# Attention before two expert layers: k and f laid out for plain transposes, values two units late

## Chip, core and metric

The kernel runs on one core of one Trainium2 chip. The metric is the device time of one execution in microseconds; for the kernel before it is 927.1 us, the median of three runs (927.02 to 927.17). A TensorE clock of 1.00 in the profile is its 2.4 GHz level, 0.50 its 1.2 GHz level.

## What is computed

Three stages in a row. Only the first is touched, apart from a small piece of work that moves out of the second.

```
f = 1 / (1 + exp(-f_logit))                      # q, k, v, f_logit: 4 batches, 8 heads, 768 steps, 48 wide
for t in range(S):                               # linear attention with a decay per head and row
    state = f[t, :, None] * state + outer(k[t], v[t])
    y[t] = q[t] @ state
logits = x @ w_gate                              # x: 3072 tokens x 384
# routing: all (token, expert) pairs in order of falling logit; a token goes to the
# first expert of its list that has fewer than 384 tokens
out[mask_e] = relu(x[mask_e] @ w1[e]) @ w2[e]    # 8 experts
# then RMS norm and a gated layer: (silu(xn @ w_gate) * (xn @ w_val)) @ w_out
```

## The kernel before

The attention stage takes the first fifth of the time. Its work is cut into 16 units, four per batch; a unit is two heads that share the 128 partitions (head 0 in rows 0 to 47, head 1 in rows 64 to 111). A head's 768 steps are six chunks of 128. The decay is handled by products of f inside a chunk: with P the running product of f and W the factor that belongs to k, the unit needs k scaled by W and q scaled by P, both with the 48 features on the partitions and the steps along the row.

The inputs arrive the other way round: `load` fetches a raw tensor as 96 partitions, each with 8 steps of both heads in contiguous runs of 1536 bytes (`raw_f`, `raw_k`, `raw_q`, three buffers each). `turned` brings them into the needed layout with TensorE: a matmul with the identity for each head and each of the 8 steps, 64 stationary columns (48 and 16 that are not used), 96 moving ones; half of a tensor fills one PSUM bank. Then come, by their names in the code: `decays` (the sigmoid of the turned f, into G and fs), `scans` (VectorE: P and W), `scale` (VectorE: kt and qt out of the turned k and q), `k_back` (five transposes of kt, copied to kn), `inner` (kt times qt for all 12 head chunks, copied to `at` on ScalarE, masked on GpSimd), `sums` (kn times v, copied to ub, state scan on VectorE into st), `values` (state and inner parts multiplied into yp0 and yp1, copied to YT). After four units `logits` and `logits_sum` do the gate. Some of the matmuls use only a part of the array: state products read 48 rows and write 48 columns (48*48 in the profile), inner values 128*48, inner products 48*128, turning 96*64, transposes the whole width.

The order of every engine is the order in which the loop at L509 and below is written out; nothing is reordered. In iteration i it turns q of unit i, runs decays of i + 2, scale and k_back of i, values of i - 1, inner of i, scans of i + 1, sums of i, and at last turns k of unit i + 1. PSUM banks for turned inputs, transposes and inner products come from one pool of five that is used in rotation (`bank()`): a new bank waits until its last reader five allocations ago is done. ScalarE and VectorE work in order, so a copy that waits holds everything behind it. Loads are issued by SyncE, also in order; each waits until its buffer has been read.

Calls in `extra` are put at the head of an iteration: constants for the routing in iteration 2, the preparation of the routing (ranges of the logits so far, two transposes) in iteration 14. In the routing stage that follows, `side` is called in each step; its first call makes more constants on GpSimd (`more_consts`) and then turns one table (`turn_inc`).

Of the kernel before, what the change touches and what calls it, by code (L numbers as in the profile page):

```python
# [63 lines left out]
class Route:  # L64
# [83 lines left out]
    def steps(self, n, rows=None, side=None):  # L148
        nc, NB, E, NA = self.tc.nc, self.NB, self.E, self.NACT
        K, ones = self.K, self.K["ones"]  # L150
        with self.tc.tile_pool(name="r_wk", bufs=2) as wk, self.tc.tile_pool(name="r_ps", bufs=2, space=PSUM) as ps:
            def one(s):
# [48 lines left out]
                if rows and s == 0:  # L201
                    side(-1)
# [103 lines left out]
def attention(tc, q, k, v, f_logit, YT, w_gate, lg, pmin, ident, extra):  # L306
# [18 lines left out]
    NR = dict(f=3, k=3, q=3)  # L325
    RAW = {}
    for nm in "fkq":
        for i in range(NR[nm]):
            t = cst.tile([TP, 2 * R * D + 16], F32, name=f"raw_{nm}{i}")
            nc.gpsimd.memset(t[:, 2 * R * D:], 20.0 if nm == "f" else 0.0)  # L330
            RAW[nm, i] = t
    NV = 4
    V = [cst.tile([128, NC, 2, D], F32, name=f"v{i}") for i in range(NV)]

# [3 lines left out]
    def load(names, i):  # L338
        if not 0 <= i < NU:
            return  # L340
        b, p = units[i]
        for nm in names:
            if nm == "v":
                for h in range(2):
                    nc.sync.dma_start(V[i % NV][:, :, h, :], v[b, 2 * p + h].rearrange("(n p) d -> p n d", p=C))
                continue
            src = dict(f=f_logit, k=k, q=q)[nm]
            nc.sync.dma_start(RAW[nm, i % NR[nm]][:, 0:2 * R * D].rearrange("p (h c) -> p h c", h=2),
                              src[b, 2 * p:2 * p + 2].rearrange("h (p r) d -> p h (r d)", r=R))
# [32 lines left out]

    def turned(nm, i, g):

        t = RAW[nm, i % NR[nm]]
        o = bank()
        for r in range(4):
            for h in range(2):
# [13 lines left out]
    def decays(i):  # L402
        G[i] = wk.tile([128, S + 1], F32, name="G")
        FS[i] = wk.tile([128, NC], F32, name="fs")
        for g in range(2):
            o = turned("f", i, g)
            nc.scalar.activation(tv(G[i][:, :S], g), ov(o), AF.Sigmoid)
            if g == 0:
                nc.scalar.activation(FS[i], o[:, 0:TP:C // R], AF.Sigmoid)
# [17 lines left out]
    def scale(O, X, F, name, i):  # L427
        X[i] = wk.tile([128, S], F32, name=name)
# [12 lines left out]
    def inner(i):  # L441

        AT[i] = wk.tile([128, 2, NC, C], F32, name="at")
# [16 lines left out]
    def sums(i):  # L460
# [6 lines left out]
        ST[i] = wk.tile([128, D, NC], F32, name="st")  # L467
# [41 lines left out]
    for i in range(-2, NU + 1):  # L509
# [12 lines left out]
        if i > -2:  # L522
            load("kq", i + 3)
        if on(i - 1):
            values(i - 1)
# [6 lines left out]
        if on(i - 1) and units[i - 1][1] == NP - 1:  # L532
            for f in (logits, logits_sum):
                for g in range(2):
                    f(units[i - 1][0], g)
        if on(i + 1):
            KO[i + 1] = [turned("k", i + 1, g) for g in range(2)]
        if i == NU - 2:
# [153 lines left out]
def tile_kernel(ctx, tc, q, k, v, f_logit, w_gate, w1, w2, w2_gate, w2_val, w2_out, rms_g, out):  # L692
# [39 lines left out]
    def prepare(bank):  # L732
# [8 lines left out]
              {2: lambda bank: K.update(route_consts(tc, rc)), 14: prepare})  # L741
# [58 lines left out]
    with ExitStack() as st:  # L800
        with tc.tile_pool(name="rw", bufs=6) as rw, tc.tile_pool(name="rwp", bufs=4, space=PSUM) as rwp:
# [7 lines left out]
            def side(s):  # L809
                if s < 0:  # L810
                    bank = rwp.tile([128, 4, 2, 64], F32, name="rows").rearrange("p a b c -> p (a b c)")
                    turn_inc(tc, K, bank[:, 0:128], ident)
                    return
                if s == 0:
                    more_consts(tc, rc, K)
# [358 lines left out]
```

## Time and profile before

| | |
|---|---|
| time, median of 3 runs | 927.1 us |
| profiled execution | 926.02 us, span 924.3 us |
| mean granted TensorE clock | 0.968 |
| TensorE busy | 876.3 us (95%) |
| VectorE, ScalarE, GpSimd busy | 502.0, 380.7, 277.3 us |
| attention stage | 0 to about 186 us |
| routing stage, clock at 0.50 | about 192 to 250 us |

The profile is of one execution, 1.1 us shorter than the median run; its span lies 1.7 us under its own time. Rows of the time line give start, length, engine, line, operation, tiles (written <- read), shapes and count, and in brackets the idle time of the engine before the row with what ended it. PE is TensorE's matmuls and PEld its weight loads. An fp32 matmul shows as two records, a transpose as one. Matmul ends are modelled and overlap, so prices are best read from start to start of neighbouring groups.

### The profile page before, as it was taken

The numbers are of one execution on the slowest core, as the hardware profiler recorded it, in microseconds if no ns is written. First come the engines' busy times: TensorE is split into PE (matmuls) and PEld (weight loads), VectorE is DVE, ScalarE is ACT, GpSimd is POOL, SyncE is SP. The second block draws the span as 40 slices with busy tenths as digits, with TensorE's granted clock in tenths as the row PEclk, the third lists the DMA queues.
The fourth block names the chain that finished last, engine by engine and source line by source line (L and its number), as shares of the span: only waits on it lengthen the run. The fifth ranks groups of instructions, "written<-read, shape, count | busy, mean of one in ns | idle before, by whom it ended". The sixth has DMA issues, their size and how long they took to land.

```text
span 924.3 us, 17642 instructions
## 1 busy us (share of the span) xinstructions
PE 876.3 (95%) x7263; PEld 844.5 (91%) x7263; DVE 502.0 (54%) x839; ACT 380.7 (41%) x748; POOL 277.3 (30%) x328
## 2 busy tenths in 40 slices
PE   7999999866699999999999999999999999999997
PEld 7889897755599999999899999999999999999996
DVE  6665666477679888886744333443324333343222
ACT  3444444366245555454752332423324232242221
POOL 3323333154557777773410201102011010100101
PEclk9999999965599999999999999999999999999999
DMA  9556551062567788776320000000000000000000
GB/s 207 122 114 135 110 119 28 1 219 109 190 243 246 248 296 290 266 243 218 104 69 1 26 1 1 27 1 26 1 1 26 1 27 2 1 26 1 26 1 26
DMA packets 70168, 87.73 MB, mean 95 GB/s; under 512 B 29632, under 2 KB 56256, under 8 KB 70080
## 3 DMA queue, kind: packets, MB, share of 16 engines
q1 hardware_dynamic: 61008, 70.00, 26.0%
q0 software_dynamic: 3072, 9.44, 3.1%
q10 hardware_dynamic: 6000, 7.09, 2.2%
q8 instruction: 58, 0.95, 0.4%
q14 instruction: 30, 0.25, 0.1%
HBM read 70.01 MB, written 16.52 MB: 94 GB/s over the span
## 4 chain that ended last, share of the span: by engine, by line
PE 71%; issue 11%; DVE 10%; POOL 3%; DMA 2%; ACT 1%; POOLq 0%; ACTq 0%; SPq 0%; DVEq 0%
PE bank L390 7%; PE yp L484 5%; PE v L574 4%; PE g L573 4%; PE v L573 4%; PE v L572 4%; PE g L574 4%; PE g L572 4%; PE o L573 4%; PE o L572 4%; PE o L574 4%; PE bank L450 3%; PE x L573 2%; PE x L574 2%; PE x L572 2%
## 5 line engine op out<-in xcount | busy, mean ns | idle before, releaser
L1112 DVE TENSOR_TENSOR hf<-sg,v 128x384 f32<-128x384 f32 x96 | 53.1, 553 | 193.8 <-PE v L574 164.6
L900 POOL TENSOR_TENSOR xlo<-xn,xhi 128x384 fp32r<-128x384 f32 x24 | 27.4, 1143 | 302.3 <-ACT xhi L899 302.3
L1115 ACT CAST hh<-hf 128x384 fp32r<-128x384 f32 x96 | 49.3, 513 | 139.0 <-DVE hf L1112 137.3
L573 PE MATMUL o<-w,hh 128*128 128x384 f32 x288 | 97.0, 337 | 0.0
L572 PE MATMUL o<-w,hh 128*128 128x384 f32 x288 | 96.6, 335 | 0.0
L573 PE MATMUL g<-xlo,w 128*128 128x384 f32 x288 | 96.6, 335 | 0.0
L574 PE MATMUL v<-xhi,w 128*128 128x384 f32 x288 | 96.6, 335 | 0.0
L572 PE MATMUL v<-xhi,w 128*128 128x384 f32 x288 | 96.6, 335 | 0.0
L573 PE MATMUL v<-xlo,w 128*128 128x384 f32 x288 | 96.5, 335 | 0.0
L574 PE MATMUL g<-xhi,w 128*128 128x384 f32 x288 | 96.5, 335 | 0.0
L574 PE MATMUL o<-w,hl 128*128 128x384 f32 x288 | 96.3, 334 | 0.0
L572 PE MATMUL g<-xhi,w 128*128 128x384 f32 x288 | 96.2, 334 | 0.0
L1110 ACT ACTIVATE sg<-g 128x384 f32<-128x384 f32 x96 | 47.1, 491 | 118.7 <-PE g L574 118.5
L1116 DVE TENSOR_TENSOR hl<-hf,hh 128x384 fp32r<-128x384 f32 x96 | 53.6, 559 | 55.6 <-ACT hh L1115 55.6
L965 POOL TENSOR_TENSOR nr<-nr,ne 128x384 f32<-128x384 f32 x36 | 62.4, 1734 | 46.5 <-DVE ne L964 17.3
L573 PE MATMUL x<-hl,w 128*128 128x384 f32 x192 | 65.7, 342 | 2.5 <-DVE hl L1037 2.2
L759 DVE TENSOR_TENSOR w<-wraw,w 128x1536 fp32r<-128x1536 f32 x35 | 64.6, 1845 | 5.3 <-ACT w L756 5.2
L572 PE MATMUL h<-xhi,w 128*128 128x384 f32 x192 | 67.1, 349 | 0.3 <-ACT xhi L928 0.3
L573 PE MATMUL h<-xlo,w 128*128 128x384 f32 x192 | 65.7, 342 | 0.0
L574 PE MATMUL h<-xhi,w 128*128 128x384 f32 x192 | 65.5, 341 | 0.0
L572 PE MATMUL x<-hh,w 128*128 128x384 f32 x192 | 65.3, 340 | 0.0
L457 POOL TENSOR_SCALAR_AFFINE_SELECT at<-at 128x384 f32<-128x384 f32 x62 | 31.5, 543 | 111.2 <-ACT at L456 111.1
(231 smaller groups left out, 2034.3 us busy)
## 6 DMA issues: line engine op xcount, KB each, us to landing
wraw<-in_moe_w_dram SPq DMA_DIRECT2D x32, 768.0 KB, 5.9
raw_f<-in_f_logit_dram SPq DMA_DIRECT2D x16, 288.0 KB, 3.4
raw_k<-in_k_dram SPq DMA_DIRECT2D x16, 288.0 KB, 5.0
raw_q<-in_q_dram SPq DMA_DIRECT2D x16, 288.0 KB, 5.0
v<-in_v_dram SPq DMA_DIRECT2D x32, 144.0 KB, 4.6
x_dram<-xrows SPq DMA_DIRECT2D x24, 192.0 KB, 1.9
nraw<-in_moe_w_gate_dram SPq DMA_DIRECT2D x12, 384.0 KB, 5.9
nraw<-in_moe_w_val_dram SPq DMA_DIRECT2D x12, 384.0 KB, 5.2
```

The lines of the kernel that those rows point to most:

```text
L390: nc.tensor.matmul(o[64 * h:64 * h + 64, r * TP:(r + 1) * TP], t[:, c0:c0 + 64], ident[0:TP, 0:TP], start=True, stop=True)
L457: nc.gpsimd.affine_select(out=t, in_=t, pattern=[[0, 3], [1, C]], compare_op=OP.is_ge, fill=0.0, base=0, channel_multiplier=-1)
L484: nc.tensor.matmul(YP[n // 3][d, (n % 3) * C:(n % 3 + 1) * C], ST[i][d, :, n] if state else V[i % NV][:, n, h, :], QT[i][d, c] if state el ...
L572: nc.tensor.matmul(out, lhs[0], rhs[0], start=first, stop=False)
L573: nc.tensor.matmul(out, lhs[0], rhs[1], start=False, stop=False)
L574: nc.tensor.matmul(out, lhs[1], rhs[0], start=False, stop=last)
L759: eng.tensor_tensor(out=lo, in0=raw, in1=hi.bitcast(F32), op=OP.subtract)
L965: nc.gpsimd.tensor_tensor(out=r, in0=r, in1=e2.bitcast(F32), op=OP.mult)
L1110: nc.scalar.activation(sg, pg, AF.Silu)
L1112: nc.vector.tensor_tensor(out=h, in0=sg, in1=pv, op=OP.mult)
L1115: nc.scalar.copy(hh, h)
L1116: nc.vector.tensor_tensor(out=hl, in0=h, in1=hh.bitcast(F32), op=OP.subtract)
```

## The change

f and k get a second layout: 96 partitions with 8 steps, each of 2 heads padded from 48 to 64 elements, so that one step of both heads is 128 columns and one plain transpose turns it. For k the load itself writes that layout (two loads of 192-byte runs, from unit 2 on; units 0 and 1 stay as before). For f the raw load stays, and a new function `relay` on ScalarE copies it through the sigmoid into the padded layout; the copies out of PSUM in `decays` become plain copies. q stays as it was. In the loop, values run for unit i - 2, at the head of the iteration, with all state products first; k and q of unit i + 1 are turned together at its end; decays move behind k_back, loads of k and q are issued one unit earlier, and the loop is one iteration longer. More buffers for qt, at and st go with that. The two small pieces of routing work move from the routing's first step into iterations 4 and 6.

```diff
+    def relay(i):
+        if 0 <= i < NU:
+            nc.scalar.activation(RL["f", i % 2][:, :, :, 0:D].rearrange("p r h d -> p h r d"),
+                                 raw("f", i)[:, 0:2 * R * D].rearrange("p (h r d) -> p h r d", h=2, r=R), AF.Sigmoid)
...
     def turned(nm, i, g):
         o = bank()
         for r in range(4):
+            if padded(nm, i):
+                t = RL[nm, i % (2 if nm == "f" else 3)]
+                nc.tensor.transpose(o[:, r * TP:(r + 1) * TP], t[:, 4 * g + r].rearrange("p h d -> p (h d)"),
+                                    ident[0:TP, 0:TP])
+                continue
...
-            nc.scalar.activation(tv(G[i][:, :S], g), ov(o), AF.Sigmoid)
+            nc.scalar.copy(tv(G[i][:, :S], g), ov(o))
...
-        todo = [(h, n, True) for h, n in ((1, 3), (0, 1), (1, 4), (0, 2), (1, 5))]
+        todo = [(h, n, True) for h, n in ((0, 1), (1, 3), (0, 2), (1, 4), (1, 5), (1, 1), (0, 3), (1, 2), (0, 4), (0, 5))]
         todo += [(h, n, False) for n in range(NC) for h in range(2)]
-        todo += [(h, n, True) for h, n in ((0, 3), (1, 1), (0, 4), (1, 2), (0, 5))]
...
+    relay(0)
+    for i in range(-2, NU + 2):
         if i in extra:
             extra[i](bank()[:, 0:256])
-        if on(i):
-            QO[i] = [turned("q", i, g) for g in range(2)]
-        if on(i + 2):
-            decays(i + 2)
-        load("f", i + 5)
+        if on(i - 2):
+            values(i - 2)
         load("v", i + 2)
         if on(i):
             scale(KO, KT, W, "kt", i)
             scale(QO, QT, P, "qt", i)
             k_back(i)
-        if i > -2:
-            load("kq", i + 3)
-        if on(i - 1):
-            values(i - 1)
+        if on(i + 2):
+            decays(i + 2)
+        load("f", i + 5)
         if on(i):
             inner(i)
         if on(i + 1):
             scans(i + 1)
         if on(i):
             sums(i)
...
         if on(i + 1):
             KO[i + 1] = [turned("k", i + 1, g) for g in range(2)]
+            QO[i + 1] = [turned("q", i + 1, g) for g in range(2)]
+        relay(i + 3)
+        load("kq", i + 4)
...
-              {2: lambda bank: K.update(route_consts(tc, rc)), 14: prepare})
+              {2: lambda bank: K.update(route_consts(tc, rc)), 4: lambda bank: more_consts(tc, rc, K),
+               6: lambda bank: turn_inc(tc, K, bank[:, 0:128], ident), 14: prepare})
```

On TensorE, in the steady part of the loop, before: U is written by sums, kt read by k_back, yp written by values.

```order
L464 MATMUL U<-v_124,kn 48x48 x10
L390 MATMUL bank<-ident,raw_k_110 64x96 x16
L390 MATMUL bank<-ident,raw_q_116 64x96 x16
L390 MATMUL bank<-ident,raw_f_108 64x96 x16
L438 MATMUL bank<-ident,kt 128x128 x5
L484 MATMUL yp_141<-qt,st 48x128
```

And now on TensorE, from the end of values to the next values; rl_f and rl_k are the padded layouts.

```order
L509 MATMUL yp_146<-at,v_127 48x128 x6
L464 MATMUL bank<-ident,kt 128x128 x5
L410 MATMUL bank<-ident,rl_f_107 128x96 x8
L476 MATMUL bank<-qt,kt 128x128 x12
L490 MATMUL U<-v_129,kn 48x48 x10
L410 MATMUL bank<-ident,rl_k_115 128x96 x8
L416 MATMUL bank<-ident,raw_q_121 64x96 x16
L509 MATMUL yp_145<-qt,st 48x128
```

f has moved from ahead of k_back to behind it, values from behind k_back to ahead of it, and k and f are 8 transposes each where they were 16 matmuls.

On ScalarE, one iteration in the steady part, before: G and fs come from decays, kn from k_back, YT from values, at from inner, ub from sums.

```order
L407 ACTIVATE G<-bank 128x96x4
L409 ACTIVATE fs<-bank 128x6
L407 ACTIVATE G<-bank 128x96x4
L439 COPY kn<-bank 128x384
L439 COPY kn<-bank 128x256
L490 COPY YT<-yp_140 112x384
L490 COPY YT<-yp_141 112x384
L456 COPY at<-bank 128x384 x4
L466 COPY ub_153<-U 128x5x48
```

The same on ScalarE now.

```order
L515 COPY YT<-yp_145 112x384
L515 COPY YT<-yp_146 112x384
L465 COPY kn<-bank 128x384
L465 COPY kn<-bank 128x256
L433 COPY G<-bank 128x96x4
L435 COPY fs<-bank 128x6
L433 COPY G<-bank 128x96x4
L482 COPY at<-bank 128x384 x4
L492 COPY ub_159<-U 128x5x48
L401 ACTIVATE rl_f_107<-raw_f_104 96x2x8x48
```

The YT copies stand first instead of behind kn, G and fs come after kn, and the relay is a new last row.

At the end of the loop on TensorE, before: one unit's values stand behind the last sums.

```order
L450 MATMUL bank<-qt,kt 128x128 x12
L464 MATMUL U<-v_125,kn 48x48 x10
L484 MATMUL yp_141<-qt,st 48x128
L484 MATMUL yp_140<-qt,st 48x128
L484 MATMUL yp_141<-qt,st 48x128
```

And now, on TensorE from the last sums to the inner part of the next values.

```order
L476 MATMUL bank<-qt,kt 128x128 x12
L490 MATMUL U<-v_130,kn 48x48 x10
L509 MATMUL yp_145<-qt,st 48x128
L509 MATMUL yp_146<-qt,st 48x128
L509 MATMUL yp_145<-qt,st 48x128
L509 MATMUL yp_146<-qt,st 48x128 x2
L509 MATMUL yp_145<-qt,st 48x128
L509 MATMUL yp_146<-qt,st 48x128
L509 MATMUL yp_145<-qt,st 48x128
L509 MATMUL yp_146<-qt,st 48x128 x2
L509 MATMUL yp_145<-at,v_129 48x128 x6
```

The values behind the last sums are now those of the unit before the last (they read v_129, not v_130), and the last unit's follow them.

## Rows read from the trace of the kernel before

**Rows 1.** Busy time by engine in one stretch: stretch, its length, busy us (instructions).

```profile
60.00:140.00 80.00, 79.85 (x1487) 70.31 (x1482) 51.54 (x74) 37.94 (x96) 26.62 (x48) 1.00 0.52 114
```

**Rows 2.** The chain of waits from 0 to 190 us, its shares by line.

```profile
by line: PE bank L390 31.9%; PE yp L484 26.1%; PE bank L450 12.3%; PE bank L438 5.9%; PE U L464 4.0%; DMA raw_f<-in_f_logit_dram 3.4%; PE bank L496 3.3%; POOL cp L179 1.3%; DVE kt L430 1.3%; PE bank L504 1.2%; ACT lgT L499 1.0%; POOL at L45
```

**Rows 3.** Time line, one unit's weight loads: start us, length us, engine, line.

```profile
118.96 0.53 PEld L438 LDWEIGHTS bank<-ident,kt 128*128 128x128 f32 x5
...
119.66 0.68 PEld L484 LDWEIGHTS yp<-qt,st 48*48 48x48 f32 x10 [0.17 <-issue]
...
120.48 1.26 PEld L484 LDWEIGHTS yp<-at,v 128*48 128x48 f32 x24
...
121.93 0.67 PEld L484 LDWEIGHTS yp<-qt,st 48*48 48x48 f32 x10 [0.18 <-issue]
...
122.75 1.42 PEld L450 LDWEIGHTS bank<-qt,kt 48*128 48x128 f32 x24
...
124.29 0.53 PEld L464 LDWEIGHTS U<-v,kn 128*48 128x48 f32 x20
...
124.73 1.36 PEld L390 LDWEIGHTS bank<-ident,raw_k 96*64 96x64 f32 x32
...
126.03 1.38 PEld L390 LDWEIGHTS bank<-ident,raw_q 96*64 96x64 f32 x32
...
127.35 1.38 PEld L390 LDWEIGHTS bank<-ident,raw_f 96*64 96x64 f32 x32
...
128.85 0.53 PEld L438 LDWEIGHTS bank<-ident,kt 128*128 128x128 f32 x5
```

**Rows 4.** Time line, the routing's first transposes, their weight loads.

```profile
185.90 1.54 PEld L556 LDWEIGHTS rows<-ident,YT 112*128 112x128 f32 x16 [0.59 <-DVE lg L505]
```

**Rows 5.** VectorE from 60 to 140 us: group, count | busy us, mean ns | idle before.

```profile
L417 DVE TENSOR_TENSOR_SCAN P<-G,d 128x768 f32<-128x768 f32 x8 | 14.1, 1758 | 0.3
...
L430 DVE TENSOR_TENSOR kt<-bank,W 128x384 f32<-128x384 f32 x16 | 8.2, 539 | 1.3 <-PE bank L390 1.1
L469 DVE TENSOR_TENSOR_SCAN st<-ub,z 128x288 f32<-128x288 f32 x8 | 7.5, 944 | 26.9 <-ACT ub L466 26.9
```

**Rows 6.** Time line, ScalarE: one G, two kn, two YT copies, one large cast.

```profile
119.08 0.49 ACT L407 ACTIVATE G<-bank 128x384 f32<-128x384 f32 x1
...
119.60 0.75 ACT L439 COPY kn<-bank 128x384 f32<-128x384 f32 x2
...
122.66 0.86 ACT L490 COPY YT<-yp 112x384 f32<-112x384 f32 x2 [2.30 <-PE yp L484]
...
196.79 1.48 ACT L822 CAST w<-wraw 128x1536 fp32r<-128x1536 f32 x1
```

**Rows 7.** DMA issues of the page: count, KB each, median us to landing.

```profile
raw_k<-in_k_dram SPq DMA_DIRECT2D x16, 288.0 KB, 5.0
...
v<-in_v_dram SPq DMA_DIRECT2D x32, 144.0 KB, 4.6
```

**Rows 8.** Time line, TensorE where it waited for VectorE in the attention stage.

```profile
33.63 0.88 PE L390 MATMUL bank<-ident,raw_f 96*64 96x96 f32 x16 [0.63 <-DVE kt L430]
...
171.94 0.74 PE L438 MATMUL bank<-ident,kt 128*128 128x128 f32 x5 [0.59 <-DVE kt L430]
...
179.43 0.89 PE L484 MATMUL yp<-qt,st 48*48 48x128 f32 x10 [1.54 <-DVE st L469]
```

**Rows 9.** The chain of waits, k_back of units 14 and 15: start, us, what.

```profile
151.41 0.70 PE bank L438 x5
...
162.74 0.73 PE bank L438 x5
```

**Rows 10.** Time line, the start on TensorE: f of unit 1, first k_back.

```profile
8.79 2.83 PE L390 MATMUL bank<-ident,raw_f 96*64 96x96 f32 x32 [1.45 <-DMA raw_f<-in_f_logit_dram]
...
16.92 0.77 PE L438 MATMUL bank<-ident,kt 128*128 128x128 f32 x5
```

**Rows 11.** Busy time by engine in the routing stage.

```profile
200.00:210.00 10.00, 5.44 (x68) 4.63 (x68) 7.94 (x29) 7.72 (x21) 5.54 (x6) 0.50 0.65 208
```

More of the change, by code (lines that the diff above doesn't have):

```diff
@@ L323, in attention, with padded, raw @@
     psl = pool("a_psl", 1, space=PSUM)
-    NR = dict(f=3, k=3, q=3)
-    RAW = {}
+    PAD = "k"
+    RAW, RL = {}, {}
     for nm in "fkq":
-        for i in range(NR[nm]):
+        for i in range(2 if nm in PAD else 3):
             t = cst.tile([TP, 2 * R * D + 16], F32, name=f"raw_{nm}{i}")
-            nc.gpsimd.memset(t[:, 2 * R * D:], 20.0 if nm == "f" else 0.0)
+            if nm != "f":
+                nc.gpsimd.memset(t[:, 2 * R * D:], 0.0)
             RAW[nm, i] = t
+        for i in range(3 if nm in PAD else 2 if nm == "f" else 0):
+            t = cst.tile([TP, R, 2, 64], F32, name=f"rl_{nm}{i}")
+            nc.gpsimd.memset(t[:, :, :, D:], 1.0 if nm == "f" else 0.0)
+            RL[nm, i] = t
+    def padded(nm, i):
+        return nm == "f" or nm in PAD and i > 1
     NV = 4
     V = [cst.tile([128, NC, 2, D], F32, name=f"v{i}") for i in range(NV)]
+    def raw(nm, i):
+        return RAW[nm, i if nm in PAD else i % 3]
     units = [(b, p) for b in range(B) for p in range(NP)]
@@ L347, in load @@
             src = dict(f=f_logit, k=k, q=q)[nm]
-            nc.sync.dma_start(RAW[nm, i % NR[nm]][:, 0:2 * R * D].rearrange("p (h c) -> p h c", h=2),
+            if nm != "f" and padded(nm, i):
+                for h in range(2):
+                    nc.sync.dma_start(RL[nm, i % 3][:, :, h, 0:D], src[b, 2 * p + h].rearrange("(p r) d -> p r d", r=R))
+                continue
+            nc.sync.dma_start(raw(nm, i)[:, 0:2 * R * D].rearrange("p (h c) -> p h c", h=2),
                               src[b, 2 * p:2 * p + 2].rearrange("h (p r) d -> p h (r d)", r=R))
@@ L427, in scale @@
     def scale(O, X, F, name, i):
-        X[i] = wk.tile([128, S], F32, name=name)
+        X[i] = wk.tile([128, S], F32, name=name, bufs=3 if X is QT else 2)
         for g in range(2):
@@ L441, in inner @@
     def inner(i):
-        AT[i] = wk.tile([128, 2, NC, C], F32, name="at")
+        AT[i] = wk.tile([128, 2, NC, C], F32, name="at", bufs=3)
         for g in range(2):
@@ L466, in sums @@
         nc.scalar.copy(UB[i % 2].rearrange("p d c -> p c d")[:, 1:], U)
-        ST[i] = wk.tile([128, D, NC], F32, name="st")
+        ST[i] = wk.tile([128, D, NC], F32, name="st", bufs=3)
         fl = "p d c -> p (d c)"
@@ L531, in attention @@
             sums(i)
-        if on(i - 1) and units[i - 1][1] == NP - 1:
+        if on(i - 2) and units[i - 2][1] == NP - 1:
             for f in (logits, logits_sum):
                 for g in range(2):
-                    f(units[i - 1][0], g)
+                    f(units[i - 2][0], g)
         if on(i + 1):
             KO[i + 1] = [turned("k", i + 1, g) for g in range(2)]
+            QO[i + 1] = [turned("q", i + 1, g) for g in range(2)]
+        relay(i + 3)
+        load("kq", i + 4)
         if i == NU - 2:
@@ L809, in side @@
             def side(s):
[L810 to L815, printed above, removed]
                 if s < 3:
```

8 lines of the change are left out of this document (3 added, 5 removed).

## The prediction

> **What bounds the kernel now.** I read the profile from the coarse to the fine. The busy times of the stretch from 60 to 140 us come first [rows 1]: TensorE is busy for 79.85 of 80 us, VectorE for 51.54, ScalarE for 37.94, GpSimd for 26.62, with the granted clock at 1.00, the 2.4 GHz level. A busy TensorE alone proves little, since pipelined matmuls overlap, so the chain of waits over the whole attention stage comes next [rows 2]: nearly all of it is TensorE (turning the raw inputs at L390 31.9%, values at L484 26.1%, inner products at L450 12.3%), and no other engine has more than a few per cent. So the loop costs what its instructions cost on TensorE. Third, the weight loads of one unit in order of time [rows 3]; their starts give the price of each group as the distance to the next group's start. From one k_back to the next it is 128.85 - 118.96 = 9.89 us: k_back 0.70, the first five state products 0.82, twelve inner values 1.45, five more state products 0.82, inner 1.54, sums 0.44, then k 1.30, q 1.32 and f 1.50 turned. The reader is to see two things there. A turned tensor is 16 matmuls of 96 columns in 1.32 us, 0.0825 us each. And f, which is the same work as q, takes 0.18 us more because a group of another tile shape follows it; the trace marks 0.17 to 0.18 us of idle time at such changes, while sums to k (128*48 to 96*64) shows none. I put a change of shape at 0.17 us. A unit of before has six of them: f to k_back, to state, to values, back to state, to inner, to sums.
>
> **The change, part by part.** All sums are against the profiled execution: 926.02 us with a span of 924.3. The median of the runs is 927.1, 1.08 above it, and I carry that difference over unchanged.
>
> *Turning.* f always, and k from unit 2 on, are turned by 8 transposes in place of 16 matmuls, each with 128 stationary and 96 moving columns. Before has no transpose of that shape. The nearest are the 16 of 112 columns at L556, whose weight loads take 1.54 us in all [rows 4]: at most 0.096 each, which by columns makes 0.0825 for 96. The other neighbour, k_back's 128 columns, is (0.70 - 0.17) / 5 = 0.106. With the last load's own length taken off L556 (about 0.1 of 1.54) the lower bound is 0.077, the upper is 0.106; I take 0.0825, since that row already has 128 stationary columns and its price per moving column, 0.86 ns, is that of the matmuls. A tensor then takes 0.66 in place of 1.32. With 14 units of k and the 14 of f that are turned at full clock: 28 x 0.66 = 18.5 us gone.
> The Trainium skill speaks against this (TensorE: Matmul & The Clock Gate, LDWEIGHTS (loading the stationary operand)): a weight load takes its column count over 1.2, so 128 columns would take 107 ns whatever the rows and the moving columns. By that, eight transposes are 0.86 and the saving is 12.9 instead of 18.5. At L556 128 columns are loaded every 96 ns or less, so the trace does not bear it out as it stands.
>
> *Order.* A steady unit is now q, values, k_back, f, inner, sums, k. By the same prices: q 1.50; ten state products 0.65 + 0.65 + 0.17 = 1.47; twelve inner values 1.45; k_back 0.53 (f's transposes have its shape); f 0.83; inner 1.54; sums 0.44 + 0.17 = 0.61; k 0.83. That is 8.76, 1.13 less than 9.89, where turning alone would give 1.32: the seventh change of shape and the rounding of these groups cost 0.19 x 13 units = 2.5 us.
>
> *Does TensorE still set the pace?* VectorE does per unit two scans of 1.76, four scalings of 0.54 and a state scan of 0.94 [rows 5]: 6.6 us, under 8.76. ScalarE does 37.94 / 80 x 9.89 = 4.7 and gets the relay, 96x768 elements. No such row exists; 384 elements take 0.49 and 1536 take 1.48 [rows 6], so 0.82 by the line between them, and never over 1.48. That makes 5.5 of 8.76. What counts is ScalarE's order after values: two YT copies (one can start when the first half of the values is in), two kn, G, fs, G, four at, ub, relay, and five PSUM banks in turn. I walked one unit through with these durations: inner's fourth bank needs the first G and fs copied. Counted from k_back's start, when the last YT copy can begin, that is 0.48 + 0.75 for two kn + 0.49 + about 0.1 = 1.8 us; TensorE gets there after k_back 0.53, f 0.83 and half of inner 0.77, 2.1 us. The cover is 0.3 us, thin; if it goes, inner's second half waits by the excess. k_back's wait for the scaled k is covered by values (2.9 us against 2.0 of scaling behind a state scan), which stand between turning and k_back now. The relay waits for f loaded three units ahead, and behind it in ScalarE's queue stands only the next unit's YT copy, over 2 us later. k in padded rows is two loads of 192-byte runs like v's, whose 144 KB land in 4.6 us where a whole raw k takes 5.0 [rows 7]; they are issued three units, some 26 us, ahead, so even twice v's time costs nothing.
>
> *Stalls that go.* At unit 1 TensorE waited 0.63 for a bank that the k scaling held [rows 8]. The iteration with the routing's preparation ran from 151.41 to 162.74 [rows 9], 11.33 where one without f needs 9.89 - 1.32 = 8.57: 2.76 lost, since the last q stood behind a transpose that waited for VectorE. Now that transpose stands behind q and ahead of values; I leave 1.0 of it, so 1.8 goes. k_back of the last unit waited 0.59, and the last values 1.54 for the state scan [rows 8]; with the values of two units left at the end, both are covered. Together 0.6 + 1.8 + 0.6 + 1.5 = 4.5 us.
>
> *Stalls that come.* Units 0 and 1 have no values to cover VectorE: unit 0 is 6.2 us on TensorE (0.53 + 0.83 + 1.54 + 0.44 + 1.32 + 1.50) against 6.6 on VectorE and the gaps between its instructions, 0.5 lost. Turning inc moves into the loop, 0.1 and a change of shape: 0.3. Together 0.8.
>
> *Start.* Before, f of unit 1 waited for its data until 8.79, and turning ran at about half the speed (2.83 for a tensor), the 1.2 GHz level; k_back began at 16.92 [rows 10]. Now the relay (0.82) stands between the data and f: f from 9.6 to 10.9, k to 13.5, q to about 15.6, k_back about 15.7 but with f of unit 2 behind it (1.5 us in before), so level. If the clock rises later, as fewer products run early, up to 3 us are lost. I take -0.5, from -3.5 to +0.5.
>
> *After attention.* The two bodies that leave the routing's first step, GpSimd constants and one transpose, stood behind that step's comparisons, and the next ones wait for VectorE's d: 0 to 0.3, taken as 0. Nothing there is tied to absolute time, so the gain of the loop arrives whole.
>
> Sum: 18.5 - 2.5 + 4.5 - 0.8 - 0.5 = 19.2 us. 926.02 - 19.2 = 906.8 for a profiled run, 907.9 for the median.
>
> **Rivals.** (1) The transposes run at the pace of their 128 stationary columns, 0.106: 28 x 8 x 0.0235 = 5.3 us less, 913.2. For it: k_back's rows. Against: the 112-column row. (2) ScalarE's burst after values sets the pace: every unit's inner waits. The YT copies moved ahead of kn and G, where before they stood behind; if each of the eight small copies comes 0.1 later than I walked, the cover of 0.3 is short by 0.5, times 13 units 6.5: 914.4. Against: before, ScalarE's copies kept their row times back to back. (3) Slower: the clock. Eight-transpose groups and k_back make 21 transposes a unit where there were five. If the granted clock fell to the 1.2 GHz level inside the loop, a unit would cost 8.8 us more; 19.2 / 8.8 = 2.2, so from three units at half clock on the change loses, and with all 14 the time is 907.9 + 14 x 8.8 = 1031. For it: between 200 and 210 us, with transposes and tiny matmuls and TensorE busy 5.44 of 10 us, the clock stood at 0.50 [rows 11]. Against: that stretch also idles nearly half the time, the loop does not, and most of a unit stays matmuls.
> The Trainium skill has this rule (TensorE: Matmul & The Clock Gate, Part 4: PE-mode transpose): transposes do not count as TensorE being busy in the way matmuls do. No row of before separates that from idling. (4) The change doesn't do what it says: every microsecond taken from TensorE comes back as a wait for another engine, and a unit stays at 9.9, 925 to 929. Against: no engine but TensorE has over 6.6 us of work in a unit.
>
> **How the numbers follow.** Forecast 0.70, with its own range from 904 to 912; rival 1 0.12, rival 2 0.13, rival 3 0.03, rival 4 0.02. The upper side takes in both waits and the late clock, so the range for 8 in 10 is 903.5 to 917. A difference under 0.2%, 1.9 us, counts as none: faster 0.95, same 0.01, slower 0.04.
>
> **What would show it.** Right: a unit of 8.7 to 8.9 us from k_back to k_back, 0.083 per transpose, TensorE still busy all through, no wait before the last values. Wrong: idle time of TensorE before inner ended by ScalarE (rival 2), transposes 0.1 apart (rival 1), a granted clock under 1.00 in the loop (rival 3), or k_back later than 18 us (the start).

## The result, and the profile after

The changed kernel takes 903.9 us (median of 4 runs, 902.40 to 904.38) against 927.1 us (4 runs, 925.81 to 927.17): a ratio of 0.9755, 95% interval 0.9743 to 0.9768. The forecast was 907.9 in a range from 903.5 to 917.0, so the gain is 23.1 us where 19.2 were worked out; the time lies 0.4 us inside the lower end of the range, and just under the 904 to 912 that the forecast had for itself. The profiled execution took 904.11 us, its span 902.4 us, with a mean granted clock of 0.966.

First, the busy times over the stretch that [rows 1] shows of before.

```profile
60.00:140.00 80.00, 79.71 (x1273) 68.38 (x1271) 55.55 (x83) 47.72 (x116) 30.30 (x54) 1.00 0.48 107
```

TensorE is still busy all through and its clock still granted at 1.00. VectorE and ScalarE have more work in the same time, since more units pass, and ScalarE has the relay besides. The chain of waits over the attention stage, its shares by line, against [rows 2]; the window is 0 to 175 us and reaches 12 us into the routing:

```profile
by line: PE yp L509 24.0%; PE bank L416 13.9%; PE bank L476 12.8%; PE bank L410 11.6%; PE bank L464 6.0%; PE U L490 4.7%; DMA raw_f<-in_f_logit_dram 3.6%; POOL cp L179 3.6%; PE bank L521 3.4%; POOL at L483 2.2%; issue 1.6%; PE bank L529 1.3
```

Turning was 31.9% at one line; now it is 13.9% (q, and k of the first two units, L416) and 11.6% (the transposes of f and k, L410) of a shorter stage. GpSimd's comparisons (L179) belong to the routing; its masks (L483) are on the chain once, from 25.46 us, which comes back below. One unit's weight loads, to be read against [rows 3] from start to start:

```profile
111.43 1.20 PEld L509 LDWEIGHTS yp<-qt,st 48*48 48x48 f32 x20
112.78 1.26 PEld L509 LDWEIGHTS yp<-at,v 128*48 128x48 f32 x24
114.22 0.53 PEld L464 LDWEIGHTS bank<-ident,kt 128*128 128x128 f32 x5 [0.19 <-ACT YT L515]
114.72 0.75 PEld L410 LDWEIGHTS bank<-ident,rl_f 96*128 96x128 f32 x8
115.58 1.42 PEld L476 LDWEIGHTS bank<-qt,kt 48*128 48x128 f32 x24
117.12 0.53 PEld L490 LDWEIGHTS U<-v,kn 128*48 128x48 f32 x20
117.71 0.70 PEld L410 LDWEIGHTS bank<-ident,rl_k 96*128 96x128 f32 x8
118.52 1.35 PEld L416 LDWEIGHTS bank<-ident,raw_q 96*64 96x64 f32 x32
119.99 1.20 PEld L509 LDWEIGHTS yp<-qt,st 48*48 48x48 f32 x20
```

The unit is 119.99 - 111.43 = 8.56 us, forecast 8.76. f is 0.86 and k 0.81, each with the change of shape behind it; the ten state products are 1.35 where I had 1.47, inner values 1.44, sums 0.59, q 1.47.

The profiled spans differ by 21.9 us (924.3 and 902.4), the medians by 23.1: the profiled run of before was 1.0 under its median, that of after 0.2 over. Of the 4.0 us by which the median came out under the forecast, some 1.2 are these two distances, since the prediction carried that of before over unchanged, and 2.7 are in the profiles. Where the 21.9 went is read by stretches between marks that both traces have: k_back of unit 2, k_back of unit 15, and the last logits' sum on VectorE. On TensorE, after, f of unit 1, q, k_back and inner of unit 0, and k_back of units 1, 2 and 15 (the first and the third to compare with [rows 10]):

```profile
9.52 1.51 PE L410 MATMUL bank<-ident,rl_f 96*128 96x96 f32 x8 [2.60 <-ACT rl_f L401]
...
13.58 2.58 PE L416 MATMUL bank<-ident,raw_q 96*64 96x96 f32 x32
16.09 0.76 PE L464 MATMUL bank<-ident,kt 128*128 128x128 f32 x5
...
17.45 1.61 PE L476 MATMUL bank<-qt,kt 48*128 48x128 f32 x24
...
22.61 0.74 PE L464 MATMUL bank<-ident,kt 128*128 128x128 f32 x5 [0.31 <-DVE kt L456]
...
32.10 0.74 PE L464 MATMUL bank<-ident,kt 128*128 128x128 f32 x5 [0.89 <-DVE kt L456]
...
150.59 0.76 PE L464 MATMUL bank<-ident,kt 128*128 128x128 f32 x5
```

And the last sum of the logits on VectorE, before and after:

```profile
185.59 0.26 DVE L505 TENSOR_REDUCE lg<-bank 128x24 f32<-128x96 f32 x1 [0.38 <-PE bank L504]
```

```profile
162.51 0.26 DVE L530 TENSOR_REDUCE lg<-bank 128x24 f32<-128x96 f32 x1 [0.44 <-PE bank L529]
```

| stretch | before | after | gained | forecast |
|---|---|---|---|---|
| start to k_back of unit 2 | 34.45 | 32.10 | 2.35 | 2.7 |
| k_back of unit 2 to that of unit 15 | 137.49 | 118.49 | 19.0 | 15.0 |
| to the last sum of the logits | 13.91 | 12.18 | 1.7 | 1.5 |
| from there to the end of the span | 738.46 | 739.63 | -1.2 | 0 |

The forecast's terms fall to the stretches so: the first has f of units 2 and 3 and k of unit 2 (3 x 0.66), the whole of f of unit 4 (1.32), which stood ahead of k_back of unit 2 and now stands behind it, the bank (0.6), and the losses 0.5, 0.5 and 0.2; the second has 24 tensors (15.8), less the 0.66 that f of unit 4 now costs there, order (-2.3), preparation and last k_back (2.4), inc (-0.3).

So the loop gained 4.0 us more than forecast. The unit is 2.4 of it, 8.56 instead of 8.76 in twelve units. The units with logits are 0.8: before, each of the three took 2.71 us more than a plain unit, now 2.43. The preparation is 0.6: it costs 0.36 where 1.0 was left standing. The first stretch gained 0.35 less than forecast.

### The profile page after: what moved, and what is told of

Read it like the earlier page. It is cut to its first block, busy times and chain, and to the rows that moved or that the text cites. A ratio compares the mean times of both kernels' runs of the same rounds, so it can differ in the third digit from the quotient of the medians.

```text
span 902.4 us, 16287 instructions
## 1 busy us (share of the span) xinstructions
PE 853.2 (95%) x6543; PEld 823.4 (91%) x6543; DVE 501.5 (56%) x839; ACT 390.3 (43%) x764; POOL 283.5 (31%) x329
## 4 chain that ended last, share of the span: by engine, by line
PE 72%; issue 11%; DVE 9%; POOL 4%; DMA 2%; ACT 1%; POOLq 0%; ACTq 0%; SPq 0%; DVEq 0%
PE yp L509 5%; PE v L599 5%; PE v L597 5%; PE g L598 5%; PE g L599 5%; PE v L598 5%; PE g L597 5%; PE o L598 4%; PE o L597 4%; PE o L599 4%; PE x L598 3%; PE bank L416 3%; PE x L599 3%; PE x L597 2%; PE bank L476 2%
## 5 line engine op out<-in xcount | busy, mean ns | idle before, releaser
L597 PE MATMUL x<-hh,w 128*128 128x384 f32 x192 | 65.4, 340 | 0.0
L599 PE MATMUL x<-hh,w 128*128 128x384 f32 x192 | 64.7, 337 | 0.0
```

Source lines behind the costliest of these rows:

```text
L597: nc.tensor.matmul(out, lhs[0], rhs[0], start=first, stop=False)
L599: nc.tensor.matmul(out, lhs[1], rhs[0], start=False, stop=last)
```

## The experiments

All of them are edits of the changed kernel; times are medians of device time, with the ratio to the kernel before from runs on the same chip. "Unit" is k_back to k_back in the steady loop, "end" the last sum of the logits in the profile (after: 8.56 and 162.77).

**One part at a time: k raw, f raw, order alone, layouts alone.** k raw sets the list of padded tensors to none:

```diff
-    PAD = "k"
+    PAD = ""
```

> The changed kernel with only k put back to raw tiles and matmuls; order of the loop, f and its relay as changed. My theory: a tensor turned by transposes costs 0.66 us less, but each change of tile shape on TensorE costs 0.17 to 0.20 us. With k raw, two changes vanish (sums to k, k to q), so a steady unit is 8.56 + 0.66 - 0.34 = 8.88 us, and 14 units cost 4.5 us: 908.4 us. Rival: changes of shape cost nothing that matters, the whole 0.66 counts: unit 9.2 us, 14 x 0.66 = 9.2 us, 913.1 us.

Measured: 908.66 us, ratio 0.9810 (0.9785 to 0.9835); unit 8.93, end 168.59. The weight loads behind sums show why k is worth only 0.37 a unit:

```profile
112.24 0.53 PEld L490 LDWEIGHTS U<-v,kn 128*48 128x48 f32 x20
112.69 1.36 PEld L416 LDWEIGHTS bank<-ident,raw_k 96*64 96x64 f32 x32
113.98 1.38 PEld L416 LDWEIGHTS bank<-ident,raw_q 96*64 96x64 f32 x32
```

sums to raw k is 0.45 instead of 0.59, and raw k to q 1.29 instead of 0.81: the transposes save 0.48 here and pay 0.14 ahead. The unit excludes the rival, which has 9.2. My theory's time came out to 0.3 us, in part by luck: in the three units with logits k raw costs 0.65, since raw k pays a change of shape behind the logits' transposes that k's own transposes do not, so attention ends 5.8 us later in the profile where 4.5 were expected, and what follows attention was 1.9 us shorter in that execution.

f raw takes the relay away and puts the sigmoid back:

```diff
-    relay(0)
...
-            nc.scalar.copy(tv(G[i][:, :S], g), ov(o))
+            nc.scalar.activation(tv(G[i][:, :S], g), ov(o), AF.Sigmoid)
...
-        return nm == "f" or nm in PAD and i > 1
+        return nm in PAD and i > 1
```

> The changed kernel with only f put back: raw tiles, matmuls, the sigmoid on the copy out of PSUM, no relay on ScalarE. Theory: 0.66 us more for each unit's f, and one more change of shape (k_back to f, 0.17 to 0.20) since raw f no longer has the shape of k_back: unit 8.56 + 0.85 = 9.4 us, 14 units 11.9 us; at the start the relay's 0.84 us goes from the path, so 903.9 + 11.9 - 0.8 = 915.0 us. Rival: the relay and ScalarE's burst cost something in every unit that the changed trace does not show as a wait, so taking f back costs less than 9 us: under 912 us.

Measured: 912.85 us, ratio 0.9851 (0.9829 to 0.9873); unit 9.37, end 172.97.

```profile
112.65 0.53 PEld L463 LDWEIGHTS bank<-ident,kt 128*128 128x128 f32 x5 [0.18 <-DVE d L444]
113.35 1.35 PEld L415 LDWEIGHTS bank<-ident,raw_f 96*64 96x64 f32 x32 [0.17 <-PE bank L463]
114.82 1.42 PEld L475 LDWEIGHTS bank<-qt,kt 48*128 48x128 f32 x24
```

f is 1.47 and k_back before it 0.70 instead of 0.50: 0.81 a unit, as the theory has it (0.85). The median lies 2 us under the theory's 915.0, and the rival's bound of 912 is under all four runs (912.54 to 915.74); the loop shows no cost of the relay. In the profile attention ends 10.2 us later where the theory has 11.1: f of unit 3 costs only 0.18, since the wait at k_back of unit 2 shrinks from 0.89 to 0.26.

Order alone is both of these edits together. Like the run behind it, it keeps the two moved pieces of routing work and the larger buffers.

> Both k and f raw and turned by matmuls as before, no relay, but the new order of the loop, values two units late, all state products first, and the two small pieces of routing work in iterations 4 and 6. Theory: five changes of shape a unit instead of six (q to state, state to inner values is one, inner values to k_back, k_back to f, f to inner, inner to sums: six, with the split of state products gone and k_back no longer next to f by its shape): unit 9.7 to 9.9 us, so only the waits of 4.5 us go, less about 1.5 us of new ones: 927.1 - 3 = 924 us, range 921.5 to 926. Rival: the order gives the part that the forecast missed (0.2 us in each unit and more at the start) by itself: 920 us or less.

Measured: 918.65 us, ratio 0.9912 (0.9889 to 0.9934); unit 9.74, end 178.56, so 7.3 us before that of the kernel before. The theory was too small and the rival's 920 is met. By stretches: 2.0 to k_back of unit 2, of which some 1.5 are f of unit 4, now behind that mark; 3.5 in the loop, so some 5.0 without that move (0.15 x 12 of the unit, the rest the preparation and the last k_back); 1.8 behind it. The unit's 0.15 is most of the 0.20 that the forecast missed in a unit, and it comes from the order, not from the layouts.

Layouts alone keep the transposes and the relay and put the loop back into the old order:

```diff
-    for i in range(-2, NU + 2):
+    for i in range(-2, NU + 1):
...
-        if on(i - 2):
-            values(i - 2)
+        if on(i):
+            QO[i] = [turned("q", i, g) for g in range(2)]
+        if on(i + 2):
+            decays(i + 2)
...
+        if on(i - 1):
+            values(i - 1)
```

> Layouts of the changed kernel (f and k by transposes, relay), but the order of before: q at the head of the iteration, decays ahead of k_back, values of unit i - 1 between k_back and inner with state products split 5 + 5. Theory: per unit f and k save 2 x 0.66, but sums to k and k to q become changes of shape and q to f is one (f to k_back none): 8 in place of 6, so 0.98 less than 9.89 = 8.9 us a unit; the waits of before for the last values and the preparation stay: about 13 x 1.0 = 13 us gained, 927.1 - 13 = 914 us. Rival: the new order is worth little beside the layouts, which alone give the 18.5 us: 908.5 us.

Measured: 918.34 us, ratio 0.9919 (0.9893 to 0.9946); unit 8.97 as expected (8.9), yet the time is 4 us over the theory, and the rival is far off. The kept profile is of the fastest of the four runs (916.11 to 920.60), so it may show less than the median lost. The waits of TensorE up to 176 us, in total, times, longest:

```profile
PE bank L410 <- DVE kt L456: 1.8, 2, 1.2
PE yp L510 <- DVE st L495: 1.5, 1, 1.5
...
PE bank L464 <- DVE kt L456: 1.0, 1, 1.0
```

The waits of the kernel before [rows 8, 9] are still there: 1.2 and 0.6 for a bank instead of 0.63, 1.41 in the preparation instead of 0.94 (below), 1.5 for the last state scan, 1.0 instead of 0.59 at the last k_back. A quicker TensorE reaches them sooner. And the clock fell, which neither before nor the changed kernel shows in the loop. TensorE around the routing's preparation:

```profile
145.12 0.88 PE L410 MATMUL bank<-ident,rl_k 96*128 96x96 f32 x8
147.40 0.78 PE L101 MATMUL bank<-ident,v 128*128 128x128 f32 x2 [1.41 <-DVE v L96]
148.12 2.83 PE L416 MATMUL bank<-ident,raw_q 96*64 96x96 f32 x32
150.88 1.33 PE L464 MATMUL bank<-ident,kt 128*128 128x128 f32 x5
```

Busy times there, the last three columns granted clock, DMA share and GB/s:

```profile
146.00:148.00 2.00, 0.58 (x2) 0.31 (x2) 1.44 (x4) 0.08 (x1) 1.85 (x3) 0.91 0.02 4
148.00:150.00 2.00, 2.00 (x25) 1.89 (x26) 1.67 (x7) 0.00 (x0) 0.47 (x2) 0.50 0.00 0
```

Ten transposes and 1.41 us of idling were all that TensorE did there between 145.1 and 148.1; then the clock stood at 0.50, the 1.2 GHz level, and q took 2.83 us instead of 1.54, k_back 1.33 instead of 0.73. In the kernel before, the wait at that place followed k turned by matmuls, and q behind it ran at its full pace, 1.54 us:

```profile
159.60 0.63 PE L101 MATMUL bank<-ident,v 128*128 128x128 f32 x2 [0.94 <-DVE v L96]
160.16 1.54 PE L390 MATMUL bank<-ident,raw_q 96*64 96x96 f32 x32
```

So the granted clock did fall inside the loop, as rival 3 of the prediction has it, but in the other order of the loop and for some 7 us, and there it cost some 2 us: k was scaled only at 150.54, so q's slowness costs 0.3, and k_back and the first two groups of values 1.6. The Trainium skill's rule that transposes do not count as TensorE being busy in the way matmuls do (TensorE: Matmul & The Clock Gate, Part 4: PE-mode transpose) fits this row; it is one occurrence, and no run here separates the transposes from the longer wait. In the changed loop, with 21 transposes a unit among its matmuls and no such wait, the granted clock stayed at 1.00.

Together the four say: alone the order is worth 8.1 us and the layouts 8.4, both 23.1. The units account for 3.4 of the missing 6.6 (layouts save 0.92 a unit in the old order, 1.18 in the new, x 13). For the rest the longer waits and the clock are enough, some 2 us each by the rows above; that is argued from one profile, not tested.

**The price of a change of shape: q turned ahead of k.**

```diff
-            KO[i + 1] = [turned("k", i + 1, g) for g in range(2)]
             QO[i + 1] = [turned("q", i + 1, g) for g in range(2)]
+            KO[i + 1] = [turned("k", i + 1, g) for g in range(2)]
```

> The changed kernel with only the order of two calls swapped: q of the next unit is turned ahead of k. The same instructions. Theory: sums to raw q is no change of shape with a price (before has that transition with no idle time), so two changes stand where three did, 0.17 to 0.20 us less a unit, 2.4 us in all: 901.5 us. Rival: a change of shape is no cost of its own but the tail of the group ahead of it, so it stays: 903.9 us; or k scaled later holds k_back: slower than 904.5 us.

Measured: 903.55 us (902.57 to 909.0), ratio 0.9770 (0.9746 to 0.9795): no change that can be told. The unit is 8.43, 0.13 shorter, a little less than a change's price:

```profile
117.47 0.53 PEld L490 LDWEIGHTS U<-v,kn 128*48 128x48 f32 x20
117.91 1.36 PEld L416 LDWEIGHTS bank<-ident,raw_q 96*64 96x64 f32 x32
```

But k is scaled later, and in the first units nothing covers that: k_back of units 0, 1 and 2 waits 0.76, 0.78 and 1.02 us for kt (after: 0, 0.31, 0.89). Theory and second rival both hold, and cancel: k_back of unit 2 comes 1.1 us later, and from there to k_back of unit 15 the loop is 1.2 shorter.

**The new waits: constants and a YT copy.** Rows of the changed trace around k_back of unit 2, all engines:

```profile
25.46 3.84 POOL L483 TENSOR_SCALAR_AFFINE_SELECT at<-at 128x384 f32<-128x384 f32 x4 [1.63 <-ACT at L482]
...
25.71 1.88 DVE L446 TENSOR_TENSOR_SCAN W<-G,d 128x768 f32<-128x768 f32 x1
...
30.45 0.31 POOL L30 IOTA edge<- 128x32 int32 x2
...
30.80 0.23 DVE L31 TENSOR_SCALAR edge<-edge 128x128 int32<-128x128 int32 x1 [2.29 <-POOL edge L30]
...
30.94 1.01 DVE L456 TENSOR_TENSOR kt<-bank,W 128x384 f32<-128x384 f32 x2
```

The routing's constants stand in GpSimd's queue behind four masks (3.84 us) and z; VectorE waits 2.29 us for one of them with the scaling of k behind it, and k_back waits for that. The kernel before has the same chain at the same unit, with VectorE's wait shorter:

```profile
32.89 0.23 DVE L31 TENSOR_SCALAR edge<-edge 128x128 int32<-128x128 int32 x1 [1.32 <-POOL edge L30]
```

This is what held the scaling of k, and with it the bank that TensorE waited for [rows 8]. The edit moves the constants to the loop's head and a copy of unit 14 to VectorE:

```diff
-              {2: lambda bank: K.update(route_consts(tc, rc)), 4: ...
+              {-1: lambda bank: K.update(route_consts(tc, rc)), 4: ...
...
-            cp = nc.vector.tensor_copy if g and i == NU - 1 else nc.scalar.copy
+            cp = nc.vector.tensor_copy if g and i >= NU - 2 else nc.scalar.copy
```

> The changed kernel with the two waits taken away that it newly shows in the attention stage: the routing's constants made at the head of the loop instead of in iteration 2, where GpSimd's masking of inner beside VectorE's scans delays them and with them k_back, and the second YT copy of unit 14 on VectorE like that of unit 15. Theory: 0.9 and 0.5 us less, attention ends at about 161.4 us instead of 162.8, time 902.5 us. Rival: the wait at k_back of unit 2 is VectorE's own amount of work in units 0 and 1, so it stays, and only 0.5 us go: attention ends at 162.3 us, or later if the constants now hold the start.

Measured: 902.56 us, ratio 0.9751 (0.9737 to 0.9764); end 161.14. k_back of unit 2 starts without a wait:

```profile
30.45 0.77 PE L464 MATMUL bank<-ident,kt 128*128 128x128 f32 x5
```

Of the 1.63 us, 0.95 is this wait; 0.69 is k_back of unit 0 at 15.40 instead of 16.09, which is the start's pace (below). The YT copy gave nothing: from unit 15's k_back to the end it is 12.17 us against 12.18; the wait is now for VectorE. So the end of attention agrees with the theory, and one of its two terms does not. The two sets of runs overlap, so the times do not tell this kernel from the changed one; the wait that went is shown by the profiles.

**ScalarE's cover.** One more copy a unit:

```diff
+        nc.scalar.copy(dup, YP[1][0:112])
```

> The changed kernel with one more copy on ScalarE in each unit, 112x384 elements (0.48 us) into a tile that nobody reads, behind the two YT copies. Theory: the changed trace has the first G and fs copied at 116.07 us and TensorE at the second half of inner, which needs their bank, at 115.58 + 0.77 = 116.35: a cover of 0.28 us. The extra copy is 0.20 us over it, so TensorE waits about 0.2 us before the second half of inner in each of some 13 units: 2.6 us, 906.5 us; the waits are ended by ScalarE at the inner products. Rival: the cover is wider than I read it (ScalarE idles over 2 us a unit), nothing waits: 903.9 us. Or narrower: 0.48 x 13 = 6.2 us, 910 us.

Measured: 907.37 us, ratio 0.9774 (0.9751 to 0.9797); unit 8.69, so 0.13 more. In the changed trace inner's two halves follow without a gap (1.54 from inner to sums); here they take 1.66:

```profile
117.45 1.54 PEld L477 LDWEIGHTS bank<-qt,kt 48*128 48x128 f32 x24
119.11 0.53 PEld L491 LDWEIGHTS U<-v,kn 128*48 128x48 f32 x20
```

On ScalarE the copies of one burst start closer together than their length:

```profile
116.62 0.48 ACT L517 COPY dup<-yp 112x384 f32<-112x384 f32 x1
116.99 0.77 ACT L466 COPY kn<-bank 128x384 f32<-128x384 f32 x2
```

The extra copy takes 116.99 - 116.62 = 0.37 us of ScalarE's time, not 0.48. It pushes what follows by 0.25: counted from the start of k_back, the first kn copy comes at 0.90 us instead of 0.65 (114.87 - 114.22 in the changed kernel, 0.50 behind the YT copy, so 0.13 were spare there). Of the 0.25 us 0.12 reach TensorE: the cover is some 0.13 us, half of the 0.28 read from the trace and of the 0.3 of the prediction. In the loop that costs 1.4 us, not 2.6; the rest of the profile's 4.1 lies at the start (0.9), in the tail (0.3, where the last values wait 0.57 for the extra copy) and behind the attention stage (1.5), where kernels scatter. That the cover is thin is shown. That inner waits for ScalarE is argued from the times, since the trace marks no wait there: fs is copied until 118.20, and the second half is due at 117.45 + 0.77 = 118.22. About half of the 0.12 already stands at the first products, behind the end of the first kn copy (117.48), a bank that the theory did not name.

**q in padded rows too.**

```diff
-    PAD = "k"
+    PAD = "kq"
```

> The changed kernel, with q treated as k is: loaded in padded rows from unit 2 on and turned by transposes. Theory: 0.66 us less a unit and one change of shape fewer (k to q): unit 8.56 - 0.66 - 0.2 = 7.7 us, 13 to 14 units give 11 to 12 us: 892.5 us. VectorE has 6.6 to 6.9 us of work a unit, so it does not decide yet. Rival: the third stream of 192-byte runs or VectorE's queue takes over (waits of TensorE before k_back ended by VectorE, or before q ended by a DMA): unit over 8.2 us, 898 us or more.

Measured: 892.28 us (891.95 to 894.14), ratio 0.9637 (0.9622 to 0.9652). The weight loads from k to values:

```profile
102.03 0.70 PEld L410 LDWEIGHTS bank<-ident,rl_k 96*128 96x128 f32 x8
102.66 0.72 PEld L410 LDWEIGHTS bank<-ident,rl_q 96*128 96x128 f32 x8
103.50 1.20 PEld L509 LDWEIGHTS yp<-qt,st 48*48 48x48 f32 x20
```

Here a group of eight transposes stands ahead of another with no change of shape: 0.63 us, 0.079 each. The next, with the change, is 0.84, so a change costs 0.2. The unit is 7.75 and the theory's time is met to 0.2 us; in the loop no wait for a load is seen, but k_back of unit 2 now waits 1.7 us for VectorE, and that of unit 15 0.6 for a YT copy.

Four more runs: this kernel once more; with both edits of the waits in it; that one once more; and with the constants in iteration 3:

> The run with q in padded rows alone once more, word for word, beside the two others on the same chip. Theory: it loses 1.7 us at k_back of unit 2 and 0.5 at the end to the waits that the other two take away: 892.3 us, 1.5 to 2 us over them. Rival: what differs between the three is smaller than what one kernel differs from run to run, and the three medians lie within 1 us.

> The changed kernel with q in padded rows and both waits taken away (routing constants at the head of the loop, second YT copy of unit 14 on VectorE). Theory: the gains add up, since they are at different places: 892.3 - 1.4 = 890.9 us, a little less since the wait of k_back of unit 2 was 1.7 us with q padded: 890.3 us. Rival: with q padded VectorE is the bound of the first units, so taking the constants away only uncovers its own work: 891.8 us or more.

> The kernel of the run with q in padded rows and both waits taken away once more, word for word. That run's profile shows TensorE at half its pace until about 23.7 us (inner of unit 0 in 2.93 us instead of 1.61), where the runs with one half of the edits have the full pace from about 15 us; its four times lie between 890.0 and 895.0. Theory: when the pace rises differs from execution to execution; with it at 15 us the attention stage ends at about 150.5 us instead of 154.4, and the median falls to 890.5. Rival: the constants on GpSimd at the head of the loop, with q's short rows loading at the same time, hold the start every time: attention ends at 154 us again, median 893 or more.

> q in padded rows, the second YT copy of unit 14 on VectorE, and the routing constants in iteration 3 of the loop instead of iteration 2 or its head. Theory: from iteration 3 on values of two units stand ahead of k_back, and GpSimd is idle for over 3 us a unit, so the constants wait for nothing and hold nothing: k_back of units 2 and 3 without a wait over 0.3 us, and nothing more at the start than in the run with q padded alone: 890.5 us. Rival: the masks of unit 2 still run at half pace beside VectorE's scans, and the constants behind them hold VectorE and with it k_back of unit 3 by 0.5 to 1 us: 891.5 us.

| | median, us | ratio to before | k_back of unit 0 / 1 / 2 | end |
|---|---|---|---|---|
| q padded, first | 892.28 | 0.9637 (0.9622 to 0.9652) | 15.58 / 22.11 / 31.61 | 152.26 |
| q padded, again | 892.98 | 0.9637 (0.9624 to 0.9650) | 16.24 / 23.23 / 32.72 | 153.37 |
| with constants at the head, first | 893.38 | 0.9622 (0.9594 to 0.9651) | 16.27 / 26.00 / 33.72 | 154.43 |
| the same, again | 891.10 | 0.9614 (0.9601 to 0.9627) | 16.53 / 23.53 / 31.25 | 151.95 |
| with constants in iteration 3 | 892.44 | 0.9633 (0.9620 to 0.9646) | 16.24 / 23.23 / 30.95 | 152.78 |

Inner of unit 0, constants at the head, first run and again:

```profile
18.81 2.93 PE L476 MATMUL bank<-qt,kt 48*128 48x128 f32 x24
```

```profile
18.49 1.61 PE L476 MATMUL bank<-qt,kt 48*128 48x128 f32 x24
```

The same kernel, the same instructions, on two chips, and unit 0 takes 9.73 us in one execution and 7.00 in the other, because TensorE's pace doubles at a different moment. The four times of the first run, all on one chip, spread as far (890.01 to 894.98). So the theory of the repetition holds in its mechanism, its 890.5 is 0.6 off, and the start alone makes 2.7 us of difference between them, more than the edit under test. The first run's theory (890.3) missed by 3.1 us; its 893.38 lies where its rival has it, but not by the rival's mechanism, since k_back of unit 2 waits for nothing there. In iteration 3 the constants hold k_back again, at unit 3:

```profile
39.87 0.74 PE L464 MATMUL bank<-ident,kt 128*128 128x128 f32 x5 [1.10 <-DVE kt L456]
```

That is the rival's 0.5 to 1 us, and its time of 891.5 is nearer than the theory's 890.5: the constants cost about 1 us at both places where GpSimd's long masks stand ahead of them. The best version is q padded with the constants at the head. From k_back of unit 1 to that of unit 2 both of its profiles take 7.72 us, and those of q padded alone 9.50 and 9.49, so 1.8 us go there each time. Whether the time falls by as much depends on the start: the repetitions, on one chip, took 889.72 to 891.99 us against 892.24 to 894.08, 1.9 between the medians, as the theory of q padded again has it, while the first two runs, on two chips, show no gain (893.38 and 892.28). Against the changed kernel it gains about 13 us.

## Why the prediction was right, and where its sizes were off

The mechanism held: TensorE sets the pace, the turned tensors cost half, and most of the old waits went. The sizes of the smaller terms were off: the loop gained 4.0 us more than worked out, and 1.2 us more behind attention, not told from scatter (below), took some of it back. That the time still lies 0.4 us inside the range is in part luck.

*Turning (18.5).* Right. Eight transposes cost 0.63 to 0.64 us, 0.079 each, where 0.0825 was taken. Rival 1 falls: k_back's 0.50 for five is 0.10 each with 128 moving columns, 0.079 with 96; both are 0.8 ns per moving column, at 128 stationary columns each time. The rule of the Trainium skill that would have made it 0.107 (TensorE: Matmul & The Clock Gate, LDWEIGHTS (loading the stationary operand)) is not borne out here.

*Order (-2.5).* The term that was most off: the unit is 8.56, not 8.76, which over 12 units is 2.4 us of the 4.0 that the loop gained beyond the forecast. I priced ten state products as twice a group of five, 0.65 each; in one group they take 1.35 with the change, 1.18 without. A change of shape costs 0.13 (q ahead of k) to 0.2 (f raw, q padded) where 0.17 was taken, and k's two changes took nearly half of its gain, as worked out.

*Stalls that go (4.5).* Three of four went; the bank's 0.6 did not (next point). Of the preparation 0.36 us is left instead of the 1.0 that I let stand. The last values no longer wait for the state scan, but for a YT copy, 0.19 us at 156.88, and moving that copy did not help.

*Stalls that come (0.8).* Unit 0 lost 0.3 rather than 0.5. What I did not see is unit 2's wait of 0.89: it is the bank's 0.63 of before in another place. I had named the scaling of k as that wait's cause and counted it as gone; behind the scaling stood GpSimd's constants, which the change does not move, and the masks ahead of them take 3.84 us beside the scans instead of 1.95.

*Start (-0.5).* Right, though k_back of unit 0 came at 16.09 instead of 16.92: f of unit 2 no longer stands ahead of it but behind it, as the prediction reckons. With both done, inner of unit 0 began at 17.45, and in the kernel before at 17.61:

```profile
17.61 1.61 PE L450 MATMUL bank<-qt,kt 48*128 48x128 f32 x24
```

These 0.16 us hold the 0.66 that f of unit 2 saves and that the sum counts under turning, so the start itself lost 0.5. Order alone, without a relay, has that k_back at 15.29. The moment at which the pace rises was rightly named as the risk; it differs between executions. The prediction calls the half pace of the start the 1.2 GHz level; the granted clock reads 1.00 there in both kernels, so no row shows that it is the clock.

*After attention (0).* The profile shows 1.2 us more. Over all fourteen profiles this stretch is 737.7 to 741.2 us and does not follow the edits; so the 1.2 is not told from scatter.

*Rivals.* ScalarE's cover is thinner than said, some 0.13 us, but holds: no unit of the changed loop waits there (rival 2). The clock stayed at 1.00 in the changed loop and fell in the layouts-alone run (rival 3). The unit did not stay at 9.9 us (rival 4).

## What to carry to other kernels

Price a new instruction from the row that shares its moving size, and add the changes of tile shape on both its sides: k, which added two, kept 0.37 us a unit; f and q, which each took one away, 0.81. Look at each layout and the order of the loop together, since the neighbours of a group decide its changes of shape, and a quicker engine uncovers the waits that the old order left; here each alone was worth some 8 us, both 23. Where TensorE does transposes and then waits, look at the granted clock of that stretch; here it fell once.

## What the runs showed of the hardware that was not expected

A mask of GpSimd that begins during a scan of VectorE is not slowed evenly but held until the scan is over. Four masks took 3.84 us from 25.46. Two of them took their usual 0.52; the other two ended 0.31 and 0.32 us behind the end of a scan, at 27.59 (the W scan, 1.88 from 25.71) and at 28.51 (the state scan, 1.00 from 27.51):

```profile
25.93 1.97 POOL L483 TENSOR_SCALAR_AFFINE_SELECT at<-at 128x384 f32<-128x384 f32 x1
...
27.86 0.97 POOL L483 TENSOR_SCALAR_AFFINE_SELECT at<-at 128x384 f32<-128x384 f32 x1
```

From 117.11 four masks took 1.94 us, with VectorE idle until 118.77:

```profile
117.11 1.94 POOL L483 TENSOR_SCALAR_AFFINE_SELECT at<-at 128x384 f32<-128x384 f32 x4 [5.20 <-ACT at L482]
```

The W scan takes 1.76 alone. The Trainium skill states that a VectorE instruction with two inputs from SBUF contends with a GpSimd one that reads SBUF (SBUF — State Buffer, Who interferes with whom). The W scan reads G and d, the state scan ub and z, and the masks read at, so the rows agree. No run here took the scans away.

TensorE's pace at the start doubles between about 14 and 24 us after the start, in the middle of a group of equal instructions, while the granted clock in the profile reads 1.00 throughout; one kernel, q padded with the constants at the head, showed both about 18 and about 24.
